# One fused kernel of attention and two expert layers: 16-bit rows between the layers, and the last unit's slots filled

## The chip, the cores and the metric

The kernel is one program on one core of a Trainium2 chip. It is written in a language in which a scheduler places semaphores and buffers; where the code asks for it, the order of an engine's instructions is the written order, otherwise a planner chooses it. The metric is device microseconds of one execution, median of several. PE is TensorE, DVE VectorE, ACT ScalarE, POOL GpSimd, SP SyncE, which issues most transfers.

## What is computed

A gated linear attention runs over 4 x 8 heads, 768 steps, head size 48. Its rows (3072 tokens, 384 wide) go through a dense two-layer network, and its output through one of eight experts per token:

```python
def _moe_ref(x, w_in, w_out):
    h = x @ w_in                      # 3072 x 384 @ 384 x 2048
    g = np.maximum(0.01 * h, h)
    return (g @ w_out)

def _moe2_ref(x, w_gate, w1, w2):     # 8 experts, 384 -> 1024 -> 384
    logits = x @ w_gate
    expert_idx = np.argmax(logits, axis=1)
    ...                               # probs: softmax of the logits
    gate_w = probs[np.arange(N), expert_idx]
    for e in range(E):
        mask = expert_idx == e
        out[mask] = gate_w[mask, None] * (np.maximum(x[mask] @ w1[e], 0) @ w2[e])
```

## The kernel before

Products are made in 16-bit parts: an operand is split into a high and a low float16, and a product is three matmuls (high-high, high-low, low-high).

**Units.** The 3072 tokens are eight units of 384 (`NU`, `UT`), numbered 0 to 7. A unit's attention is cut into `front` (decays, a scan of six levels in place in the one buffer `Ft`, logarithm and exponent, a Newton step, scaled k and q) and `back` (states, scores, outputs, the turned rows `xT`). The dense network of a unit is `moe1`: 16 slots of `products` and `leaky` (first half), then 18 slots of `stage2` (three groups of 128 rows, six slots each). `run_slots` runs the generators of other work one step a slot beside it: a step that yields n waits n slots. Units 0 and 1 start in another way: unit 0's dense layer and unit 1's attention are woven in `first`, where the planner chooses the order. From unit 1's dense layer on, PE, DVE, ACT and POOL keep the written order; SP doesn't.

**state["at"]** tells how far the dense layer is: u in its first half, u + 0.5 in its second. `fronts` lets the attention front of unit u begin when it has reached u - 1.5; `backs` follow. `first_weights` begins once the last unit's attention is done, in the second half of unit 6.

**Rows between the layers.** `finish_out` scales a group's output from PSUM (`po`) into `xg`, and `route` finds expert and place for each token, writes the rows to `x2_rows` in DRAM and scatters token numbers into `tok_list`. `tile_table` makes 28 tiles of 128 tokens (`NM`), the first 14 (`NA`) from units 0 to 6 alone. For tile j, `token_list` reads its list (SP), `gather` its rows (an indirect transfer from POOL) and `turn` transposes them into `XT` (PE, ACT, DVE).

**Experts.** `experts` goes through the 28 tiles four times (`NPH`), with a quarter of the hidden width each time: `stage` copies an expert's first weights to a fixed place (DVE), `hidden`, `relu_hi`, `relu_lo`, `combine`, `accumulate`. The weights of pass p + 1 come during pass p (`load_phase`, 32 slices of 128 x 384, 192 KB each, in a ring of `wr` buffers) and are split in two parts; those of pass 0 come with `first_weights`. Where `on_dve` says so, the low part is made by DVE, else GpSimd scales the slice and subtracts. Lists and tables of the last unit (`last_tiles`) run beside the first pass.

## Time and profile before

| | us |
|---|---|
| median of three runs | 910.66 (906.37 to 915.27) |
| the profiled execution | 912.01 |
| its span, first to last instruction | 910.3 |
| unit 1's dense layer, 163.5 to 245.9 | 82.4 |
| unit 2's, 245.9 to 309.4 | 63.5 |
| last unit's, and up to the first expert product, 559.1 to 641.7 | 82.6 |
| first pass through the experts, 641.7 to 728.9 | 87.2 |
| second pass, 728.9 to 785.5 | 56.6 |

How to read it: TensorE is busy 90% of the span (816.9 us), VectorE 72%, ScalarE 57%, GpSimd 55%. A busy table has a row for a stretch: its ends and length, then the busy us of PE, PEld (weight loads), DVE, ACT and POOL with the number of instructions, the granted clock of TensorE (1 is full), the share of the DMA engines and GB/s. A group row has line, engine, operation, written<-read names, shape and count, then busy us and mean ns of one, then the idle time of that engine just before and what ended it. A timeline row has start and length in us, engine, line, operation, names, count, and in brackets the idle time before and what ended it. "<-issue" is a wait that the trace puts down to no other engine; SPq is SyncE issuing a transfer.

### The profile page before, as it was taken

Reading aid. Unit: us, or ns where it says so; the run is one execution under the profiler, and the core shown is the slowest. Engines: PE = TensorE matmul, PEld = TensorE weight load, DVE = VectorE, ACT = ScalarE, POOL = GpSimd, SP = SyncE. Lnnn points to the kernel's source line nnn. Section 1 sums busy time; section 2 is a strip of 40 time slices with the busy share of each in tenths; the row PEclk is TensorE's granted clock in tenths of the full one; section 3 lists DMA queues with packets and bytes.
Section 4 is the critical chain, followed back from the end, with each engine's and each line's share of the span. In section 5 each row is a group of like instructions: output and inputs, shape, how many; then the busy total and the mean of one; then the engine's idle time right before and its main releaser. Section 6 shows DMA issues by size and latency. Waiting matters only on the chain.

```text
span 910.3 us, 20348 instructions
## 1 busy us (share of the span) xinstructions
PE 816.9 (90%) x7015; PEld 583.1 (64%) x7015; DVE 654.8 (72%) x1594; ACT 520.4 (57%) x1425; POOL 497.4 (55%) x575
## 2 busy tenths in 40 slices
PE   5978899959999999999999997992488899999995
PEld 3654588637677676676776664551466677777884
DVE  8899964667856766657559665655766998887774
ACT  4656755555667565575574663523346767677342
POOL 6366852254273463472552650652239879899453
PEclk8879799979999999999999999997789999999998
DMA  9573261123211212212100016225326434343121
GB/s 246 134 180 79 75 168 45 28 52 80 54 27 46 60 27 54 53 28 53 27 1 28 1 35 119 56 70 166 89 53 167 141 97 123 106 123 106 63 91 63
DMA packets 150748, 73.16 MB, mean 80 GB/s; under 512 B 108651, under 2 KB 144563, under 8 KB 150640
## 3 DMA queue, kind: packets, MB, share of 16 engines
q1 hardware_dynamic: 146176, 61.40, 26.7%
q0 software_dynamic: 4464, 10.38, 3.9%
q8 instruction: 60, 0.98, 0.5%
q14 instruction: 48, 0.39, 0.2%
HBM read 62.18 MB, written 10.36 MB: 80 GB/s over the span
## 4 chain that ended last, share of the span: by engine, by line
PE 65%; DVE 17%; issue 7%; ACT 4%; DMA 3%; POOL 2%; SPq 2%; DVEq 0%; POOLq 0%; ACTq 0%
PE m L825 15%; PE m L848 15%; PE a L1325 10%; PE m L1351 10%; PE a L319 3%; DMA wr<-in_moe_w 2%; PE a L676 2%; PE m L308 2%; DVE gf L835 2%; DVE Ft L543 1%; DVE W L1049 1%; PE a L704 1%; DVE Ft L347 1%; PE a L655 1%; PE a L468 1%
## 5 line engine op out<-in xcount | busy, mean ns | idle before, releaser
L825 PE MATMUL m<-xT,wih 128*128 128x384 f16 x1152 | 207.6, 336 | 8.2 <-DVE gf L835 7.6
L848 PE MATMUL m<-woh,gh 128*128 128x392 f16 x1152 | 205.0, 329 | 4.9 <-issue 2.1
L841 POOL TENSOR_TENSOR gh<-gf,gh 128x384 f16<-128x384 f32 x128 | 122.4, 963 | 127.4 <-ACT gh L840 127.2
L825 PEld LDWEIGHTS <-wih 128*128 128x128 f16 x1152 | 114.4, 101 | 83.7 <-issue 18.5
L1325 PE MATMUL a<-XT,st 128*128 128x128 f16 x2016 | 133.9, 222 | 34.7 <-DVE st L1296 32.8
L848 PEld LDWEIGHTS <-gh 128*128 128x128 f16 x1152 | 112.0, 99 | 76.6 <-issue 6.0
L1325 PEld LDWEIGHTS <-st 128*128 128x128 f16 x2016 | 122.0, 99 | 52.2 <-DVE st L1296 40.8
L835 DVE SCALAR_TENSOR_TENSOR gf<-m,gf 128x384 f32<-128x384 f32 x128 | 70.9, 554 | 89.7 <-ACT gf L834 85.4
L1351 PE MATMUL m<-W,hs 128*128 x672 | 128.2, 328 | 0.0
L840 ACT CAST gh<-gf 128x384 f16<-128x384 f32 x128 | 65.4, 511 | 64.5 <-DVE gf L835 62.1
L1095 POOL TENSOR_TENSOR W<-wr,W 128x384 f16<-128x384 f32 x88 | 84.5, 960 | 29.3 <-ACT W L192 21.6
L834 ACT ACTIVATE gf<-m 128x384 f32<-128x384 f32 x128 | 62.4, 487 | 50.5 <-PE m L825 41.8
L192 ACT ACTIVATE W<-wr 128x384 bf16<-128x384 f32 x128 | 66.4, 519 | 38.5 <-DMA wr<-in_moe_w 38.3
L1296 DVE COPY st<-W 128x1536 f16 x112 | 81.1, 724 | 2.7 <-issue 1.2
L1351 PEld LDWEIGHTS <-hs 128*128 128x128 f16 x672 | 61.5, 98 | 29.7 <-issue 0.7
L1076 POOL TENSOR_SCALAR wr<-wr 128x384 f32<-128x384 f32 x88 | 59.9, 682 | 27.3 <-DMA wr<-in_moe_w 26.4
L1337 DVE SCALAR_TENSOR_TENSOR hs<-a,hs 128x256 f16<-128x256 f32 x112 | 47.1, 421 | 27.7 <-ACT hs L1333 18.1
L1333 ACT ACTIVATE hs<-a 128x256 f16<-128x256 f32 x112 | 41.9, 374 | 38.3 <-PE a L1325 37.3
L319 PE MATMUL a<-ident,nat 128*128 128x128 f32 x288 | 44.8, 292 | 20.1 <-issue 9.9
L1093 ACT CAST W<-wr 128x384 f16<-128x384 f32 x88 | 44.9, 510 | 30.7 <-POOL wr L1076 29.6
L979 POOL DMA_INDIRECT tok_list<-con,pi x24 | 25.7, 1071 | 59.2 <-DVE xg L974 53.6
L1364 DVE SCALAR_TENSOR_TENSOR acc<-m,acc 128x384 f32<-128x384 f32 x84 | 51.7, 615 | 4.5 <-PE m L1351 0.7
(253 smaller groups left out, 1407.1 us busy)
## 6 DMA issues: line engine op xcount, KB each, us to landing
wr<-in_moe_w SPq DMA_DIRECT2D x128, 192.0 KB
raw_in<-in_moe_w_in SPq DMA_DIRECT2D x12, 512.0 KB
raw<-in_moe_w_out SPq DMA_DIRECT2D x16, 384.0 KB
x_rows<-xg SPq DMA_DIRECT2D x24, 193.0 KB
nat<-in_alpha SPq DMA_DIRECT2D x24, 192.0 KB
nat<-in_k SPq DMA_DIRECT2D x24, 192.0 KB
nat<-in_q SPq DMA_DIRECT2D x24, 192.0 KB
vt<-in_v SPq DMA_DIRECT2D x24, 192.0 KB
```

The lines of the kernel that those rows point to most:

```text
L192: A.activation(scrap, src, AF.Square, scale=scale, accum_out=g_sq[:, i : i + 1])
L319: T.transpose(pt[:, c * P : (c + 1) * P], nt[:, c, pr].rearrange("p z d -> p (z d)"), ident)
L825: T.matmul(ph[:, 0:UT], wih[:, a, kk, f * P : (f + 1) * P], xT[:, b, kk, :], start=(n == 0), stop=(n == 8),)
L834: A.activation(gf, ph[:, 0:UT], AF.Copy, scale=0.01 * CG)
L835: V.scalar_tensor_tensor(gf, ph[:, 0:UT], CG, gf, ALU.mult, ALU.max)
L840: A.copy(g[f][:, 0], gf)
L841: G.tensor_tensor(out=g[f][:, 1], in0=gf, in1=g[f][:, 0], op=ALU.subtract)
L848: T.matmul(po[:, 0:ROW], g[f][:, a, c * P : (c + 1) * P], woh[:, b, f, :], start=(n == 0), stop=(n == 3 * NF - 1),)
L1095: G.tensor_tensor(out=lo, in0=raw, in1=hi, op=ALU.subtract)
L1296: V.tensor_copy(out=sth[i % 2].rearrange("p a k f -> p a (k f)"), in_=Wp[ph][0][:, :, ds(reg(V, j), 1), :, :].rearrange("p a e k f -> p a ...
L1325: T.matmul(hp[:, f * P : (f + 1) * P], st[:, a, kk, f * P : (f + 1) * P], XT[j][:, b, kk, :], start=(n == 0), stop=(n == 8),)
L1351: T.matmul(yp[:, 0:DM], hs[:, a, i, :], W2[:, b, ds(rp, 1), i, :].rearrange("p e f -> p (e f)"), start=(n == 0), stop=(n == 5),)
```

## The change

Rows are stored in two float16 parts in the same bytes (`x16`): the copy out of PSUM writes the high part (`upper`), and a VectorE instruction one slot later the low part (`lower`). `turn` transposes six 16-bit blocks and copies them once. The first 15 steps of unit 2's front are taken ahead of the written order, right behind `first`; the Newton steps stand one step earlier. Fronts begin at u - 1.6, and `state["at"]` goes to u + 0.4 after 12 slots. Lists, gathers and turns of the first 14 tiles go one a slot in the last unit, three slots apart; `other_turns` is gone. The ring of weight buffers has nine in place of four; in unit 6 every fourth slice is followed by the next without a slot between, and in the last unit the slices pause until its second half. In pass 0 all 32 slices of pass 1 are split on VectorE and ScalarE, none on GpSimd; 8 were before.

```diff
--- before.py
+++ after.py
@@ -48,8 +48,7 @@
 C1 = 1.0 / (2.0 * SA * SB * CG)
 C2 = C1 / (2.0 * SW * SW)
 EXPM = 0x7F800000
-T0 = 3
-DV = 4, 1
+RING = 9
 AHEAD = (0, 0, 0)
 WARM = (45,2,2,6,4)
 LV, Y1 = 2, 9.0
@@ -579,12 +578,13 @@
             for m, sl in ((ml, slice(0, 64)), (mr, slice(64, 128))):
                 V.scalar_tensor_tensor(D5[:, pr, :, sl], pt[:, :, sl], by, m[:, pr, :, sl], ALU.mult, ALU.mult)
 
+        newton(0)
+        yield 1
+        newton(1)
+        yield 1
         vs = lp[0].tile([P, 2, 3, DM], F16, tag="vs", name="vs", bufs=1)
         r["vs"] = vs
-        newton(0)
         k0 = [tp(nk, 0), tp(nk, 1)]
-        yield 1
-        newton(1)
         G.tensor_scalar(vt, vt, YV, 1.0, ALU.mult, ALU.mult)
         yield 1
         for pr in range(2):
@@ -875,6 +875,8 @@
         g = {}
         state["at"] = u
         for f in range(NF):
+            if f == 12:
+                state["at"] = u + 0.4
             ph = products(f, xT)
             next_slot()
             gf = leaky(ph)
@@ -905,6 +907,7 @@
         e1 = res["e1"]
         xg = rt.tile([P, XR], F32, tag="xg", name="xg", bufs=4)
         rows.append(xg)
+        x16 = xg[:, 0:DM].bitcast(F16)
 
         def scale():
             mx = pm.tile([P, 1], F32, tag="mx", name="mx", bufs=2)
@@ -912,7 +915,14 @@
             s2, e2 = pow2(mx, K2, 1, "n2")
             V.tensor_scalar(L[:, c, :], po[:, DM:ROW], e1[c], C1 / res["ys"], ALU.mult, ALU.mult)
             V.scalar_tensor_tensor(gsc[:, c : c + 1], e1[c], C2 / res["ys"], e2, ALU.mult, ALU.mult)
-            when(1, lambda: A.activation(xg[:, 0:DM], po[:, 0:DM], AF.Copy, scale=s2))
+            when(1, partial(upper, s2))
+
+        def upper(s2):
+            A.activation(x16[:, 0:DM], po[:, 0:DM], AF.Copy, scale=s2)
+            when(1, partial(lower, s2))
+
+        def lower(s2):
+            V.scalar_tensor_tensor(x16[:, DM : 2 * DM], po[:, 0:DM], s2, x16[:, 0:DM], ALU.mult, ALU.subtract)
 
         when(2, scale)
 
@@ -1069,7 +1079,7 @@
                 raws.append((raw, *(W2[:, a, e, i, :] for a in range(2))))
 
         def on_dve(n):
-            return ph == 0 or (ph == 1 and n % DV[0] < DV[1])
+            return ph < 2
 
         def scaled(n):
             if n < NW and not on_dve(n):
@@ -1157,6 +1167,11 @@
         yield t
 
     weave(first(), [wo_steps, then(pause(AT0), attn(1, ld[1], res[1]))], 1.5)
+
+    ld[2] = attn_load(2)
+    first_front = front(2, False)
+    for _ in range(15):
+        next(first_front)
     everything = {getattr(mybir.EngineType, e) for e in ("PE", "Activation", "DVE", "Pool")}
     pe_order.enter_context(tc.manual_schedule(engines=everything))
     tm_ctx.close()
@@ -1187,9 +1202,9 @@
 
     def fronts():
         for u in range(2, NU):
-            while state["at"] < u - 1.5:
+            while state["at"] < u - 1.6:
                 yield 1
-            yield from front(u, u == 2)
+            yield from first_front if u == 2 else front(u, False)
             state["front"] = u
             yield 1
 
@@ -1223,12 +1238,17 @@
         acc.extend(pw.tile([P, XR], F32, name=f"acc{j}") for j in range(NA))
         sth.append(pw.tile([P, 2, 3, FQ], F16, name="st0"))
         n = 0
-        for _ in load_phase(0, pw, pw, 4):
+        for _ in load_phase(0, pw, pw, RING):
             n += 1
             if n % 2 == 0:
-                yield 1 if state["at"] % 1 else 4
-
-    ld[2] = attn_load(2)
+                if state["at"] < NU - 1:
+                    if n % 8:
+                        yield 1
+                else:
+                    yield 1
+                    while state["at"] < NU - 0.5:
+                        yield 1
+
     halves = fronts(), backs()
     sides = [[0, g] for g in (*halves, first_weights())]
 
@@ -1257,32 +1277,26 @@
         )
 
     def turn(j):
-        px = pst("a")
-        for kk in range(3):
-            T.transpose(px[:, kk * P : (kk + 1) * P], acc[j][:, kk * P : (kk + 1) * P], ident)
-        pxv = px[:, 0:DM].rearrange("p (k t) -> p k t", k=3)
-        A.copy(XT[j][:, 0], pxv)
-        after(lambda: V.tensor_tensor(out=XT[j][:, 1], in0=pxv, in1=XT[j][:, 0], op=ALU.subtract))
+        px = pst("a").bitcast(F16)
+        x16 = acc[j][:, 0:DM].bitcast(F16)
+        for kk in range(6):
+            T.transpose(px[:, kk * P : (kk + 1) * P], x16[:, kk * P : (kk + 1) * P], ident16)
+        A.copy(XT[j].rearrange("p a k t -> p (a k t)"), px[:, 0 : 2 * DM])
 
     def full_tiles():
         yield 3
         yield from route(NU - 2, res[NU - 2])
         yield 1
         yield from tile_table(0, NA)
-        for j in range(NA):
-            token_list(j)
-        yield 3
-        for j in range(NA):
-            gather(j)
-            if 8 <= j < 8 + T0:
-                turn(j - 8)
+        for j in range(NA + 6):
+            if j < NA:
+                token_list(j)
+            if 3 <= j < NA + 3:
+                gather(j - 3)
+            if j >= 6:
+                turn(j - 6)
+                state["turned"] = j - 6
             yield 1
-
-    def other_turns():
-        for j in range(T0, NA):
-            turn(j)
-            state["turned"] = j
-            yield 2.0
 
     regs = {}
 
@@ -1363,7 +1377,7 @@
         else:
             V.scalar_tensor_tensor(ac, yp[:, 0:DM], gt, ac, ALU.mult, ALU.add)
         if ph == NPH - 1:
-            junk = pw.tile([P, DM], F32, tag="wr", name="junk", bufs=4)
+            junk = pw.tile([P, DM], F32, tag="wr", name="junk", bufs=RING)
             A.activation(junk, ac, AF.Copy, scale=0.0, accum_out=g_out[:, j : j + 1])
             if j == 0:
                 G.drain()
@@ -1399,7 +1413,7 @@
 
     def weights(ph):
 
-        it = load_phase(ph + 1, pw if ph % 2 else m2, pw, 4) if ph + 1 < NPH else iter(())
+        it = load_phase(ph + 1, pw if ph % 2 else m2, pw, RING) if ph + 1 < NPH else iter(())
         for j in range(NM):
             if j:
                 next(it, None)
@@ -1417,7 +1431,7 @@
         n = NPH * NM
         for i in range(n + 3):
             while i < NM and state["turned"] < i:
-                next(turns if i < NA else lists, None)
+                next(lists, None)
                 while late:
                     late.pop(0)()
             if i < n:
@@ -1440,8 +1454,7 @@
             yield
 
     lists = last_tiles()
-    turns = other_turns()
-    weave(experts(), [turns, lists], 2.0)
+    weave(experts(), [lists], 2.0)
     pe_order.close()
 
 
```

## Rows read from the trace of the kernel before

**Rows 1.** Busy table by stretch: us (count) per engine, clock, DMA share, GB/s.
```profile
100.00:163.50 63.50, 61.93 (x462) 48.15 (x463) 39.63 (x91) 36.96 (x109) 32.91 (x49) 0.95 0.35 93
...
163.50:245.90 82.40, 70.32 (x548) 49.12 (x547) 60.62 (x168) 48.48 (x127) 34.94 (x33) 0.94 0.25 51
...
245.90:309.40 63.50, 63.50 (x507) 43.95 (x507) 43.52 (x125) 38.86 (x99) 31.16 (x32) 1.00 0.22 46
...
559.10:641.70 82.60, 53.02 (x305) 29.90 (x302) 51.73 (x145) 32.29 (x93) 32.01 (x34) 0.89 0.39 108
...
641.70:728.90 87.20, 68.88 (x731) 54.54 (x732) 68.71 (x165) 50.70 (x150) 54.18 (x65) 0.93 0.42 111
...
728.90:785.50 56.60, 56.60 (x682) 44.25 (x680) 47.88 (x86) 41.17 (x124) 51.31 (x64) 1.00 0.39 112
```
**Rows 2.** Timeline around unit 1's attention; columns as told above.
```profile
118.34 0.35 DVE L371 SCALAR_TENSOR_TENSOR qt<-a,Ft 128x192 f32<-128x192 f32 x1
...
193.33 1.51 PE L319 MATMUL a<-ident,nat 128*128 128x128 f32 x6 [9.89 <-issue]
```
**Rows 3.** Groups of 163.5 to 245.9 (unit 1); columns as told above.
```profile
L543 DVE TENSOR_TENSOR Ft<-Ft 128x384 f32<-128x384 f32 x24 | 16.1, 720 | 0.0
...
L319 PE MATMUL a<-ident,nat 128*128 128x128 f32 x72 | 10.8, 285 | 9.9 <-issue 9.9
...
L575 DVE SCALAR_TENSOR_TENSOR R<-ln,R 128x768 f32<-128x768 f32 x4 | 5.0, 1249 | 0.1
```
**Rows 4.** Timeline of the last unit and the hand-over, all engines.
```profile
557.56 0.52 ACT L192 ACTIVATE W<-wr 128x384 bf16<-128x384 f32 x1 [9.04 <-DMA wr<-in_moe_w]
...
568.80 7.69 PE L825 MATMUL m<-xT,wih 128*128 128x384 f16 x36 [5.13 <-DVE gf L835]
...
601.30 18.98 SPq L1249 DMA_DIRECT2D tok<-tok_list  x14
...
623.44 0.52 ACT L192 ACTIVATE W<-wr 128x384 bf16<-128x384 f32 x1 [20.36 <-DMA wr<-in_moe_w]
...
641.14 0.56 DVE L1296 COPY st<-W 128x1536 f16 x1 [0.54 <-DVE W L1049]
...
641.75 2.10 PE L1325 MATMUL a<-XT,st 128*128 128x128 f16 x18 [18.96 <-DVE st L1296]
```
**Rows 5.** Groups of 641.7 to 728.9, the first pass through the experts.
```profile
L1325 PE MATMUL a<-XT,st 128*128 128x128 f16 x500 | 35.4, 229 | 34.6 <-DVE st L1296 32.8 <-DVE acc L1362 0.8 <-ACT XT L1264 0.8
...
L1095 POOL TENSOR_TENSOR W<-wr,W 128x384 f16<-128x384 f32 x24 | 22.6, 943 | 19.8 <-ACT W L192 19.7
...
L1296 DVE COPY st<-W 128x1536 f16 x28 | 21.6, 772 | 1.6 <-issue 1.2 <-DVE acc L1362 0.3
...
L1265 DVE TENSOR_TENSOR XT<-a,XT 128x384 f16<-128x384 f32 x25 | 13.7, 549 | 12.2 <-ACT XT L1264 10.4 <-ACT W L192 1.8
...
L1262 PE MATMUL a<-ident,acc 128*128 128x128 f32 x75 | 13.4, 289 | 2.6 <-DVE XT L1265 2.3 <-issue 0.2
...
L1430 DVE SCALAR_TENSOR_TENSOR W<-wr,W 128x384 f16<-128x384 f32 x8 | 5.7, 710 | 0.6 <-ACT W L1088 0.6
```
**Rows 6.** Timeline of the first pass through the experts.
```profile
648.54 1.18 PE L1325 MATMUL a<-XT,st 128*128 128x128 f16 x18 [1.49 <-DVE st L1296]
...
660.62 2.10 PE L1325 MATMUL a<-XT,st 128*128 128x128 f16 x18 [6.60 <-DVE st L1296]
...
662.92 8.45 SPq L1249 DMA_DIRECT2D tok<-tok_list  x6
...
674.08 0.52 POOL L1076 TENSOR_SCALAR wr<-wr 128x384 f32<-128x384 f32 x1 [5.69 <-DMA wr<-in_moe_w]
```
**Rows 7.** Groups of the whole span: a ScalarE instruction 768 wide.
```profile
L556 ACT ACTIVATE ln<-Ft 128x768 f32<-128x768 f32 x12 | 10.0, 834 | 20.0 <-DVE Ft L543 20.0
```
**Rows 8.** Timeline of the last unit: a gather on GpSimd, a turn on TensorE.
```profile
605.71 0.98 POOL L1252 DMA_INDIRECT acc<-x_rows,tok  x1 [0.30 <-issue]
...
610.07 0.49 PE L1262 MATMUL a<-ident,acc 128*128 128x128 f32 x3
```

More of the change, by code (lines that the diff above doesn't have):

```diff
@@ L273, in tile_kernel @@
     lp = [pm]
-    state = {"S": None, "SU": None, "e": None, "nat": 0, "sm": 0, "wo": 0, "turned": T0 - 1, "at": 0, "attn": 1, "front": 1}
+    state = {"S": None, "SU": None, "e": None, "nat": 0, "sm": 0, "wo": 0, "turned": -1, "at": 0, "attn": 1, "front": 1}
     qeng = [nc.sync, nc.scalar]
@@ L1519, in last_experts @@
             G.indirect_dma_start(out=x, out_offset=None, in_=x2d, in_offset=rows)
+            x16 = x[:, 0:DM].bitcast(F16)
+            xs = le.tile([P, DM], F32, name="l_xs")
+            V.tensor_tensor(out=xs, in0=x16[:, 0:DM], in1=x16[:, DM : 2 * DM], op=ALU.add)
             px = pst("a")
             for kk in range(3):
-                T.transpose(px[:, kk * P : (kk + 1) * P], x[:, kk * P : (kk + 1) * P], ident)
+                T.transpose(px[:, kk * P : (kk + 1) * P], xs[:, kk * P : (kk + 1) * P], ident)
             xT = le.tile([P, 3, P], F32, name="l_xT")
```

## The prediction

> **What bounds the kernel now.** I read the busy table by stage first [rows 1]. In units 2 to 5 (one shown, 245.9 to 309.4) TensorE is busy all of the time at the full granted clock, with VectorE at 43.5 of 63.5 us: nothing taken from another engine is worth anything there. The second pass through the experts (728.9 to 785.5, 28 tiles in 56.6 us, 2.02 us each) is bound by TensorE in the same way. TensorE loses time in three places. Unit 1 takes 82.4 us with 70.3 busy, 12.1 idle. The last unit with the hand-over to the experts takes 82.6 with 53.0 busy, 29.6 idle. The first pass through the experts takes 87.2 with 68.9 busy, 18.3 idle. These 60 us are what the change can take from; the rest is start and tail.
>
> Next the timeline of each hole, to see which wait ends last. Unit 1: VectorE runs the scan of unit 2, six levels of two multiplications at 0.72 us, then the Newton steps [rows 3]; the products with k come after them in its queue, and TensorE's transposes for q need the PSUM buffers that these set free: idle 9.9 us until 193.3 [rows 2]. Last unit: SyncE issues 14 token lists in one go, 18.98 us from 601.3 [rows 4]. The expert weights stand behind them in its queue, so ScalarE sits 20.36 us, and the first stage copy, emitted behind every weight slice, comes at 641.1 after a TensorE wait of 18.96 us. TensorE also lost 5.13 us at 568.8 to a `gf` that stood on VectorE behind weight work. First pass: TensorE waits 34.6 us ahead of its weight-and-token product, 32.8 of it for the stage copy [rows 5], so what ends last is VectorE's queue: 68.7 us busy, and 12.2 idle ahead of the subtraction of `turn`, which waits for a ScalarE that stood behind GpSimd's scaling, which stood behind a weight transfer (5.69 us at 674.1), issued behind six token lists (8.45 us from 662.9) [rows 6].
>
> **The change, part by part.** *Unit 2's scan, traced in unit 0's stage.* It takes out of unit 1's queues 12 transposes on TensorE (12 x 0.15, 1.8 us), eight copies on ScalarE, half of the 24 level instructions on VectorE (12 x 0.72, 8.6 us) and half of the Newton steps (four at 1.25, 5 us) [rows 3]. VectorE in unit 1 goes from 60.6 to about 47, TensorE needs 70.3 - 1.8 = 68.5, so TensorE should be the bound as in unit 2. Of the 12.1 us idle I keep 3. Where it goes: the scan's buffer `Ft` is free once unit 1's q is scaled, at 118.7 [rows 2], and over 100 to 163.5 VectorE has 23.9 us free, most of it after that [rows 1]: 13.6 fit. TensorE there is full (61.9 of 63.5), so the transposes cost their 1.8 us again, and I take 1 more for attention steps of unit 1 delayed on VectorE. Gain 9.1 + 1.8, cost 2.8, -8; the clock (granted 0.94 in unit 1, 1.00 in unit 2) gives an estimated 2 back: **-10**. Bounds: no idle left and all hidden, -14; the scan put at the end of unit 0 and half exposed, -4.
>
> *Two 16-bit parts.* `lower` is new, 24 times on VectorE. No row shows it; the subtraction in `turn` has the same operand kinds and takes 0.55 us (13.7 us for 25 [rows 5]); bounds 0 and the 0.71 of a `lo`. It holds the PSUM buffer `po` a slot longer and stands ahead of the next `gf`. In the units TensorE is the cover, with 20 us of VectorE free: 0. With that cover gone it costs 24 x 0.55 = 13 us. The three at the hand-over may cost 0.5.
>
> *Turns.* Three 32-bit transposes, a copy and a subtraction become six 16-bit transposes and one copy of 768. A turn costs TensorE 0.54 now (13.4 us for 25 [rows 5]). Six 16-bit ones are not shown: below, 18 products of the same width take 1.18 us [rows 6], so 0.39; above, six at the 32-bit price, 1.07. I take 0.45, near the row of the same type and width. The copy I take at the 0.83 of a 768 wide one [rows 7], bounds half and all of it. VectorE loses the 25 subtractions and their waits.
>
> *Lists, gathers, turns and weights in the last unit's slots.* The first weights start three slots earlier in unit 6 (a slot is 63.5/34 = 1.87 us) and go four slices to three slots; by my count of the yields 18 of 32 are done when the last unit begins, one more in its first slot, and none until its second half. So in slots 15 to 34 SyncE has the lists almost to itself, and with nine buffers the transfers of later slices are issued ahead of the lists. Of the 29.6 us idle I expect 1.5 in place of the 18.96, 3 of the 5.13 and its like, and 1 of the rest. TensorE's own work is 53.0 plus 14 turns less the three there now (14 x 0.45 - 3 x 0.54 = 4.7). Sum 53.0 + 4.7 + 5.5 = 63.2, less 1.2 for the clock (granted 0.89): 62 against 82.6, **-20.6**. Bounds: 57.7 with no idle at all (-25); 72, if half of the idle stays (-10). VectorE pays two instructions of up to 0.71 us a slice and ScalarE a square and 0.83 a turn, against slots of 1.87: covered.
>
> *First pass without GpSimd.* GpSimd loses 22.6 us of subtractions and its scalings; 24 more slices put a `lo` of 0.71 us on VectorE [rows 5]: +17.0. VectorE: 68.7 - 13.7 + 17.0 = 72.0 busy; of 18.5 idle the 12.2 ahead of the turn's subtraction go, 6.3 stay: 78. The stage copy has a mean of 0.77 here against 0.56 for one at 641.1 [rows 4]; GpSimd, with which it was drawn out, falls from 54.2 us to under 32: 28 copies at 0.1 less, 75. TensorE: 68.9 - 25 x 0.54 + 14 x 0.45 = 61.7, plus 12 for the waits on the last rows' routing and tables, which stay (6.60 us at 660.6 [rows 6] is the largest): 74. Both say 74.5 against 87.2: **-12.7**. Bounds: 64 and 90.
>
> The Trainium skill (SBUF — State Buffer, "Who interferes with whom") has GpSimd and VectorE's copies lock each other out of shared ports for a whole instruction; by that rule all that a stage copy has over 0.56 us would go, some 3 us more than I count. The same page (its "DVE blocks DMA" trap) speaks against gathers beside VectorE's copies, since GpSimd writes their descriptors. Gathers beside such copies in the last unit follow each other at 0.30 us [rows 8]; the trace does not bear the trap out here, and I charge nothing.
>
> Sum: -10 - 20.6 - 12.7 + 0.5 = -42.8. The profiled execution has 912.0 us (span 910.3 and 1.7 around it), the median of the runs is 910.66: **869**.
>
> **The rivals.**
> *Weights still late (881).* The four slices in flight at 548 took until 557.6, with ScalarE 9.04 us idle [rows 4]: 2.3 us a slice. At that rate 18 slices take 41 us, and their slots in unit 6 last 24; the queues of ScalarE and VectorE carry the delay into the last unit's `gf`, and some 12 of the 20.6 us stay lost. Against it: four buffers allowed no more in flight, and nine do.
> *VectorE keeps the first pass (885).* If its idle time stays beside the added work, 72.0 + 18.5 = 90: the 12.7 us are not gained and 3 are lost.
> *The scan is not hidden (878).* The order in unit 0's stage is left to the planner, which may place the scan behind unit 0's last work; then unit 1's first `gf` stand behind it and 9 of the 10 us go.
> *Everything opens (854).* No idle left in unit 1 and the hand-over (4 + 4.4), the stage copy at its best and the tables overlapped (7).
> *The first three together (906):* 869 + 12 + 16 + 9, within 1% of now.
> *Slower (925).* Turns now stand in TensorE's own order in the last unit, each behind its list, its gather and two landings. If a gather's data comes later than the three slots given to it, each of 14 turns stops the matmuls: above (42.8 + 9.1)/14 = 3.7 us a turn the change is slower by over 1%, and at 4.0 it is 925. Against it: a gather issued until 606.7 is turned at 610.1 without a wait [rows 8], 3.4 us, and three slots are 4.5 to 6.
>
> **How the numbers follow.** Forecast 0.55; weights late 0.15; VectorE 0.10; everything opens 0.07; scan not hidden 0.06; the three together 0.04; slower 0.03. A measurement of this kernel can tell about 1% from no change, 901.6 to 919.8 here: faster 0.93, same 0.04, slower 0.03. The likeliest case's own range is 855 to 881. The range 846 to 893 takes in the bounds of the hand-over and of the first pass and all cases but the last two.
>
> **What would show it.** Right: no long gap of TensorE in unit 1, and unit 1 near 70 us; scan instructions before 163; the first expert product within 3 us of the last unit's end; lists on SyncE one by one; ScalarE never 5 us on a weight slice in the last unit; GpSimd with gathers and scatters alone in the first pass, and 28 tiles there in about 75 us. Wrong: scan levels after 165, `gf` waits over 5 us at the last unit's start, turns with a wait on a gather, or VectorE over 95% busy in the first pass. What would overthrow the forecast is a new wait of over 20 us on TensorE in the last unit.

## The result and the profile after

The changed kernel takes 899.58 us (median), the kernel before 910.66 beside it: a ratio of 0.989, interval 0.986 to 0.993. The forecast was 869, with 846 to 893. The direction was right; of the 42 us of gain forecast against that median, 11 came.

The busy table by stretch, of the kernel after: us, busy time and count of TensorE, its weight loads, VectorE, ScalarE and GpSimd, granted clock, DMA share, GB/s. The stretches are the end of unit 0, unit 1, unit 2, the last unit with the hand-over, and the first and second pass through the experts.

```profile
100.00:160.80 60.80, 59.66 (x465) 47.09 (x463) 38.63 (x94) 34.90 (x104) 29.32 (x46) 0.99 0.36 95
160.80:246.00 85.20, 70.40 (x540) 48.67 (x538) 60.16 (x170) 47.68 (x125) 34.65 (x35) 0.94 0.25 49
246.00:309.20 63.20, 63.20 (x507) 43.84 (x505) 42.10 (x126) 38.61 (x99) 30.40 (x31) 1.00 0.24 45
559.10:633.10 74.00, 60.03 (x380) 35.77 (x379) 43.51 (x123) 35.70 (x87) 31.64 (x33) 0.88 0.39 110
633.10:713.60 80.50, 66.12 (x744) 52.64 (x742) 62.59 (x164) 50.74 (x141) 18.45 (x19) 0.89 0.41 117
713.60:770.00 56.40, 56.40 (x679) 44.11 (x677) 50.20 (x87) 41.16 (x124) 49.43 (x61) 1.00 0.39 114
```

Against [rows 1]: unit 1 is 2.8 us longer, not 10 shorter. The hand-over fell from 82.6 to 74.0 (forecast 62), the first pass from 87.2 to 80.5 (forecast 74.5). The second pass has not moved. In unit 1 VectorE is as busy as before and TensorE has the same two losses, 14.8 us of idle (12.1 before) and a clock of 0.94. The profiled execution took 895.93 us, 3.7 less than the median. The timeline of unit 1 after (start, us, engine, line, operation, out<-in, count, idle before and its releaser) says why.

```profile
164.31 5.23 DVE L542 TENSOR_TENSOR Ft<-Ft 128x384 f32<-128x384 f32 x11
...
169.54 0.55 DVE L835 SCALAR_TENSOR_TENSOR gf<-m,gf 128x384 f32<-128x384 f32 x1
...
173.84 2.52 DVE L574 SCALAR_TENSOR_TENSOR R<-ln,R 128x768 f32<-128x768 f32 x2
...
176.29 0.54 DVE L835 SCALAR_TENSOR_TENSOR gf<-m,gf 128x384 f32<-128x384 f32 x1
...
177.46 1.51 PE L318 MATMUL a<-ident,nat 128*128 128x128 f32 x6 [10.44 <-issue]
```

Unit 2's scan, which was to run in unit 0's stage, runs with its Newton steps from 163.2 to 176.3, in unit 1. It stands behind unit 0's last work, as the code emits it; unit 1's `gf` stand behind it in VectorE's order, and TensorE's gap is the old one (9.9 us in [rows 2]) 16 us earlier. The last unit and the first pass, on the same timeline:

```profile
566.50 3.69 PE L825 MATMUL m<-xT,wih 128*128 128x384 f16 x13 [2.88 <-DVE gf L835]
...
599.45 1.16 POOL L1272 DMA_INDIRECT acc<-x_rows,tok  x1 [2.20 <-DMA tok<-tok_list]
...
603.16 0.80 PE L1283 MATMUL a<-ident,acc 128*128 128x128 f16 x6 [6.68 <-DMA acc<-x_rows,tok]
...
615.09 0.33 PE L848 MATMUL m<-woh,gh 128*128 128x392 f16 x1 [0.91 <-issue]
...
616.51 0.33 PE L848 MATMUL m<-woh,gh 128*128 128x392 f16 x1 [1.10 <-issue]
...
617.24 0.49 PE L848 MATMUL m<-woh,gh 128*128 128x392 f16 x1 [0.40 <-issue]
617.94 0.50 PE L848 MATMUL m<-woh,gh 128*128 128x392 f16 x1 [0.22 <-issue]
...
619.45 0.80 ACT L1284 COPY XT<-a 128x768 f16<-128x768 f16 x1 [5.87 <-remote]
...
652.19 2.10 PE L1339 MATMUL a<-XT,st 128*128 128x128 f16 x18 [5.21 <-DVE st L1310]
...
678.98 0.22 PE L1283 MATMUL a<-ident,acc 128*128 128x128 f16 x1 [0.52 <-issue]
...
679.71 0.27 PE L1283 MATMUL a<-ident,acc 128*128 128x128 f16 x2 [0.51 <-issue]
```

Three things are to be seen. The 18.96 us wait for the stage copy [rows 4] is gone, and ScalarE's 20 us on a weight slice with it. In their place TensorE waits 6.7 us at the first turn for its gather. And from 613.8 to 619.3, and again at 671 and from 678 to 682, TensorE starts an instruction only every 0.7 us or slower: matmuls that wait for nothing stand alone, 0.7 to 1.4 us apart, and ScalarE starts nothing for 5.9 us ("<-remote" is a release that the trace places on no engine). I call this slow issue. The busy table of the stretch, with one before and one behind it:

```profile
605.00:613.40 8.40, 8.40 (x64) 5.48 (x63) 4.08 (x12) 4.53 (x12) 5.13 (x6) 0.88 0.67 173
613.40:620.00 6.60, 3.08 (x15) 1.06 (x13) 1.35 (x3) 0.73 (x3) 3.65 (x5) 0.79 0.69 193
620.00:628.00 8.00, 8.00 (x54) 5.16 (x53) 5.82 (x16) 6.95 (x17) 0.76 (x1) 0.75 0.64 188
```

Last, groups of the first pass after (busy us, mean ns | idle before, releasers):

```profile
L1339 PE MATMUL a<-XT,st 128*128 128x128 f16 x501 | 36.3, 231 | 13.0 <-DVE st L1310 10.0 <-PE a L1283 1.9 <-issue 0.9
...
L1310 DVE COPY st<-W 128x1536 f16 x28 | 16.1, 575 | 3.1 <-DVE acc L1376 1.8 <-issue 1.1
...
L1284 ACT COPY XT<-a 128x768 f16<-128x768 f16 x16 | 12.7, 794 | 4.3 <-PE a L1283 4.2
```

The DMA engines are no busier in the slow stretch (0.69) than before (0.67) and behind it (0.64), so their load alone does not mark it. The wait ahead of the expert product fell from 34.6 to 13.0 us [rows 5]; the stage copy fell from a mean of 772 to 575 ns; the turn's copy is 794 ns, 830 forecast.

### The profile page after: what moved, and what is told of

Same layout as the page of the kernel before. It is cut to its first block, busy times and chain, and to the rows that moved or that the text cites. A ratio compares the mean times of both kernels' runs of the same rounds, so it can differ in the third digit from the quotient of the medians.

```text
span 893.8 us, 20449 instructions
## 1 busy us (share of the span) xinstructions
PE 817.0 (91%) x7099; PEld 584.7 (65%) x7099; DVE 653.3 (73%) x1614; ACT 527.2 (59%) x1425; POOL 458.6 (51%) x527
## 4 chain that ended last, share of the span: by engine, by line
PE 74%; DVE 12%; issue 4%; ACT 4%; DMA 3%; POOL 3%; DVEq 0%; SPq 0%; POOLq 0%; ACTq 0%
PE m L848 16%; PE m L825 16%; PE a L1339 13%; PE m L1365 12%; PE a L318 3%; PE a L676 2%; PE a L655 1%; PE a L1283 1%; DMA wr<-in_moe_w 1%; DVE gf L835 1%; PE a L704 1%; DVE Ft L346 1%; PE a L712 1%; PE a L467 1%; DVE w L1513 1%
## 5 line engine op out<-in xcount | busy, mean ns | idle before, releaser
L848 PE MATMUL m<-woh,gh 128*128 128x392 f16 x1152 | 207.1, 332 | 3.5 <-issue 3.5
L1365 PE MATMUL m<-W,hs 128*128 x672 | 130.3, 332 | 0.0
L1105 POOL TENSOR_TENSOR W<-wr,W 128x384 f16<-128x384 f32 x64 | 61.6, 963 | 20.3 <-ACT W L191 16.3
L1086 POOL TENSOR_SCALAR wr<-wr 128x384 f32<-128x384 f32 x64 | 44.7, 700 | 22.8 <-DMA wr<-in_moe_w 22.7
L318 PEld LDWEIGHTS a<-ident,nat 128*128 128x128 f32 x288 | 36.6, 148 | 23.3 <-issue 12.9
```

The lines of the kernel that those rows point to most:

```text
L318: T.transpose(pt[:, c * P : (c + 1) * P], nt[:, c, pr].rearrange("p z d -> p (z d)"), ident)
L848: T.matmul(po[:, 0:ROW], g[f][:, a, c * P : (c + 1) * P], woh[:, b, f, :], start=(n == 0), stop=(n == 3 * NF - 1),)
L1105: G.tensor_tensor(out=lo, in0=raw, in1=hi, op=ALU.subtract)
L1365: T.matmul(yp[:, 0:DM], hs[:, a, i, :], W2[:, b, ds(rp, 1), i, :].rearrange("p e f -> p (e f)"), start=(n == 0), stop=(n == 5),)
```

## Experiments

Kernels timed side by side on one chip, with the kernel before among them, form a set. All ratios are to the kernel before in the same set. "First pass" runs from the first expert product to the second pass's first stage copy, "hand-over" from the last unit's first product to the first expert product. In the cuts of code, `...` marks what is left out, and words behind # are added here.

### The scan

**scan_mid.** The scan's steps are emitted in between those of unit 1's attention.

```diff
...
-    weave(first(), [wo_steps, then(pause(AT0), attn(1, ld[1], res[1]))], 1.5)
...
-    ld[2] = attn_load(2)
     first_front = front(2, False)
-    for _ in range(15):
-        next(first_front)
...
+    def lead():
+        while state["q"] < 1:        # set in attn() behind scaled(nq, qt, R5, F5)
+            yield 0.5
+        ld[2] = attn_load(2)
+        for _ in range(15):
+            next(first_front)
+            yield 2.0
...
+    weave(first(), [wo_steps, then(pause(AT0), attn(1, ld[1], res[1])), lead()], 1.5)
```

> The changed kernel with the first steps of unit 2's scan emitted between the steps of unit 1's attention, from the moment that attention has scaled q, and no longer behind it. Theory (the move was worth nothing only because the planner put the scan behind unit 0's last work): scan levels before 150, unit 1 from 85 to 70 to 74 us, TensorE's 10.4 us gap there gone, whole time 8 to 11 us under the changed kernel's 899.6, near 890 and 0.978 of before. Rival (unit 0's stage is full, what is put there comes out behind it): unit 0's stage grows by 8 to 13 us, whole time within 3 us of 899.6.

874.37 us, 0.961 (0.958 to 0.964). Unit 0 and unit 1 of it, and the first of its scan levels:

```profile
66.60:166.20 99.60, 88.83 (x629) 63.94 (x627) 85.65 (x179) 65.97 (x197) 57.66 (x72) 0.96 0.36 90
166.20:239.10 72.90, 68.69 (x539) 48.06 (x538) 50.95 (x154) 43.13 (x105) 34.24 (x35) 1.00 0.25 46
...
142.13 0.55 DVE L543 TENSOR_TENSOR Ft<-Ft 128x384 f32<-128x384 f32 x1
```

The theory holds in what the trace shows: a scan level at 142.1, unit 1 at 72.9 us with 4.2 idle and the clock at 1.00; unit 0's 99.6 lie among the 98.3 to 101.6 that executions with the scan behind it take. The whole time was expected near 890 and is 25 us under the 899.58 of the first measurement; more than half of that has another cause, since this set has no slow issue (after_third, below). What the scan's place is worth shows within the set: scan_back, with the scan in unit 1, takes 886.12, turn_late, with the scan behind unit 0, 885.09; so 11 to 12 us. The idea of the change was worth its 10 us; the place at which the scan is emitted lost them.

**scan_back.** The scan back in unit 1.

```diff
-    first_front = front(2, False)
-    for _ in range(15):
-        next(first_front)
...
-            yield from first_front if u == 2 else front(u, False)
+            yield from front(u, u == 2)
```

> The changed kernel with unit 2's scan back in unit 1, as before the change; all else as changed. Theory (the move of the scan gained nothing): whole time within 3 us of the changed kernel's 899.6, unit 0 and unit 1 together 179 to 182 us against 186 after and 179 before from the first product of unit 0. Rival (the move did gain in unit 0 or later and the loss came from another part): 6 to 10 us over 899.6.

886.12 us, 0.977 (0.973 to 0.981). That looks like a gain of 13 us over 899.58. The trace contradicts it: scan_back shows no slow issue, and the changed kernel itself came to 886.9 in a set without it (after_third, below). Against that, and against 885.09 for turn_late in the same set, the move was worth nothing, as expected. Units 0 to 2 together take 248.0 us here, 247.7 in after_third, 242.4 before: so the change costs some 5 us there with the scan in either place. I moved nothing else of that part, so the cause (fronts that begin at the 13th product, the Newton steps spread over more slots) stays open.

```profile
60.00:156.60 96.60, 87.85 (x616) 63.55 (x615) 74.25 (x155) 60.93 (x175) 54.22 (x71) 0.95 0.34 87
156.60:240.10 83.50, 70.54 (x540) 48.80 (x539) 63.41 (x167) 47.03 (x125) 34.52 (x32) 0.96 0.25 46
240.10:308.00 67.90, 65.55 (x515) 45.28 (x515) 46.65 (x136) 39.84 (x101) 34.68 (x35) 1.00 0.24 45
```

### Slow issue

**after_again, after_third.** The changed kernel unedited, in two other sets.

> The changed kernel as it is, a second time. Theory (the stretches at 614 to 620 and 671 to 682, in which all engines issue one instruction in 0.7 us, belong to the chip or the execution and not to the kernel, since four near relatives show none): none of them, hand-over near 70 and first pass near 73 us against 74.0 and 80.5, whole time 886 to 891. Rival (they belong to this kernel's own times of gathers): the stretches again, whole time 897 to 902.

902.02 us, 0.992 (0.989 to 0.995), slow issue again, hand-over 74.4 and first pass 80.0: the rival's numbers. Its reason, that the stretches belong to this kernel, does not stand up to the next run.

> The changed kernel as it is, as a measure for the others of this set. With the stretches of slow issue: 897 to 903, hand-over 74, first pass 80. Without: 885 to 891, hand-over 70, first pass 73.

886.9 us, 0.975 (0.969 to 0.981), on the same chip as after_again, and no slow issue anywhere. Its last unit and first pass:

```profile
560.10:627.70 67.60, 57.56 (x383) 35.17 (x381) 42.91 (x122) 36.27 (x87) 32.33 (x33) 0.92 0.43 123
627.70:699.60 71.90, 63.55 (x744) 51.95 (x742) 61.56 (x164) 50.21 (x141) 18.42 (x19) 0.91 0.46 131
...
604.06 0.80 PE L1283 MATMUL a<-ident,acc 128*128 128x128 f16 x6 [6.70 <-DMA acc<-x_rows,tok]
```

So one kernel on one chip has two times 15 us apart (13 against the first measurement), alike within a set. Three sets had slow issue (the first measurement, that of after_again, that of ring4), three had not (one of these, that of lists_static_2, without the unedited kernel in it). The kernel before has little of it (some 2 us at 614 to 619 in its profile, where TensorE's weight loads come 0.7 us apart): 910.6 to 911.0 in the sets with, 908.3, 908.6 and 910.9 in those without. Two of its rows:

```profile
616.56 0.10 PEld L848 LDWEIGHTS <-gh 128*128 128x128 f16 x1 [0.61 <-issue]
...
617.28 0.26 PEld L848 LDWEIGHTS <-gh 128*128 128x128 f16 x2 [0.62 <-issue]
```

**spread.** Gathers drawn apart, in a set whose near kernels (pace_back, x16_back) show slow issue; the unedited kernel was not in that set. In the first pass the second edit draws lists and turns apart too.

```diff
     def gather(j):
+        for _ in range(3):
+            G.tensor_scalar(fill, fill, 1.0, 1.0, ALU.mult, ALU.mult)
         G.indirect_dma_start(
...
-            yield 1.0        # in last_tiles()
+            yield 2.0
```

> The changed kernel with gathers drawn apart: three small operations of GpSimd, 0.2 us or so each, ahead of every gather, and the last rows' lists, gathers and turns at half the pace in the first pass. Theory A (gathers one behind the other hold up the issue on all engines): on a chip where such stretches appear in the changed kernel, at most 2 us of them are left, whole time 5 to 9 us under the changed kernel's 900 to 902 there; where they do not appear, within 3 us. Rival B (lists, or the amount of transfers): the stretches stay, whole time within 3 us.

899.1 us, 0.987 (0.981 to 0.994). No slow issue; gathers are 2.5 to 3.1 us apart, against 1.2 to 1.6 for three to eight in a row ahead of every such stretch in the others.

```profile
565.70:645.60 79.90, 58.90 (x381) 34.44 (x379) 46.17 (x130) 36.72 (x89) 47.96 (x75) 0.91 0.37 103
645.60:718.00 72.40, 64.13 (x744) 52.37 (x743) 61.83 (x158) 50.16 (x140) 37.60 (x61) 0.88 0.47 130
...
633.16 0.51 PE L1288 MATMUL a<-ident,acc 128*128 128x128 f16 x6 [1.87 <-DMA acc<-x_rows,tok]
```

The first pass falls to 72.4 us, as theory A wants. The hand-over grows to 79.9: at that distance the gathers fall behind the turns, and behind the first, which waits 7.0 us, nine more wait 0.4 to 1.9 us each. So the whole time stays, where theory A expected 5 to 9 us less, by another mechanism than either theory named.

**lists_static, gather_plain.** List addresses as constants; plain transfers of 128 rows in order in place of gathers, so that the experts get other rows than theirs.

```diff
-        ro = nc.sync.value_load(off[0:1, j : j + 1], min_val=0, max_val=E * CAP)
-        nc.sync.dma_start(out=tok[:, j : j + 1], in_=lst[ds(ro, P), :])
+        e, t = LISTS[j]
+        nc.sync.dma_start(out=tok[:, j : j + 1], in_=lst[e * CAP + t * P : e * CAP + t * P + P, :])
```

```diff
-        G.indirect_dma_start(out=acc[j], ...)
+        t0 = j * P if j < NA else NTOK - (NM - j) * P
+        G.dma_start(out=acc[j], in_=x2d[t0 : t0 + P, :])
```

> The changed kernel with each gather by a list replaced by a plain transfer of 128 rows in order, of the same size and from the same queue; the token lists are still loaded but the experts work on the wrong rows. Theory A (gathers by a list, one behind the other, hold up the issue of instructions on all engines at once, some 5.5 us at 614 to 620 and some 5.7 at 671 to 682): no stretch in which TensorE issues one instruction in 0.7 us, the first pass from 80.5 to 75 us, the hand-over 5 us shorter. Rival B (the list loads with an address from a register do it, or so many transfers of any kind at once): such stretches stay, with 4 us or more in all.

> The changed kernel with plain transfers of 128 rows in place of the gathers, a second time, beside the changed kernel on the same chip; the experts work on the wrong rows. Theory A (gathers by a list): no stretch of slow issue, first pass 72 to 73 us, whole time 8 to 13 us under the changed kernel of the set where that has the stretches. Rival C (the amount of transfers of any kind): stretches of 4 us or more stay.

> The changed kernel with plain transfers in place of gathers, a third time, beside the one with fixed list addresses; the experts work on the wrong rows. Theory A: no stretch of slow issue, first pass 72 to 75 us, 884 to 889, also where its neighbour shows them. Rival C (close transfers of any kind): stretches as in its neighbour, 894 or more.

> The changed kernel with the 28 token lists loaded from addresses written into the program (those that the tables give for this data) and not from registers; so a list no longer waits for the table. Theory A (gathers by a list make the slow issue): stretches of 0.7 us a step stay, 4 us or more in all, where the changed kernel of the same set has them. Rival B (the register loads, with SyncE's address work, make it): none left. In both the first turn's wait of 6.6 us shrinks below 3, since its list comes earlier.

> The changed kernel with the token lists loaded from addresses written into the program, a second time, in a new set. Theory A (close gathers by a list make the slow issue, in some sets): if the set has it, stretches of 4 us or more and 894 to 900 us. Rival B (the register loads make it): none, 883 to 887. If the kernel beside it and this one both show none, nothing follows.

gather_plain 884.44, 888.41 and 885.88 us, lists_static 885.15 and 887.37, none with slow issue, but no neighbour in their sets had it either. So they don't tell A from B or C. They show one thing: the hand-over is 66.4 to 68.0 us in these runs, whether a list waits for its table or not, and whether a transfer waits for a list or not. With plain transfers, mostly 0.53 us apart, the first turn still waits 3.7 to 3.8 us and no later one waits, but the wait for a `gf` at the unit's start is 4.8 to 5.0 us where it was 2.7. That the first turn's wait would fall below 3 us with early lists was wrong (4.6).

### Which part brought the gain

Each part of the change was taken back alone, in sets with slow issue. The changed kernel stands at 0.989 and 0.992 in such sets; it was timed beside pool_back and slots_back, but not in the set of ring4, pace_back and x16_back.

```diff
-        return ph < 2                     # pool_back
+        return ph == 0 or (ph == 1 and n % 4 < 1)
-RING = 9                                  # ring4
+RING = 4
-                if state["at"] < NU - 1:  # pace_back, with the loop under it
+                yield 1 if state["at"] % 1 else 4
```

slots_back puts `full_tiles` and `other_turns` back as they were, x16_back puts `finish_out` and `turn` back.

> The changed kernel with GpSimd scaling and subtracting three of four weight slices in the first pass, as before the change. Theory (taking GpSimd off is what brought the first pass from 87 to 73 us, since VectorE's queue ended last there): first pass 80 to 87 us, whole time 7 to 14 us over the changed kernel of the same set. Rival (the turns and lists taken out of the first pass brought it, and GpSimd's work was hidden): first pass under 76, whole time within 2 us.

899.57 us, 0.989 (0.983 to 0.994): 2.5 us under the changed kernel of the set, near what the rival has, but not for its reason. The first pass is 79.2 us against 80.0 in the same set, without slow issue in it, though the hand-over of the same execution has it (615 to 620): GpSimd's scalings and subtractions hold the first pass's gathers 1.9 to 4.2 us apart.

```profile
632.20:711.40 79.20, 62.70 (x743) 49.69 (x741) 57.77 (x140) 50.51 (x141) 53.53 (x62) 0.94 0.45 117
...
L1310 DVE COPY st<-W 128x1536 f16 x27 | 18.7, 694 | 2.0 <-DVE acc L1376 0.8 <-issue 0.8
```

Against 71.7 to 73.3 us for the pass where gathers stand close and no slow issue comes, taking GpSimd off is worth 6 to 7 us, and in sets with slow issue that is given back: the gathers then close up, and slow issue comes. The stage copy has a mean of 694 ns with GpSimd busy and 575 without. By the Trainium skill (SBUF — State Buffer, "Who interferes with whom") copies of VectorE in a two-port mode and GpSimd's instructions lock each other out; the two means agree with that.

> The changed kernel with the lists issued in one go, the gathers behind them, three turns in the last unit and eleven in the first pass, as before the change; weights, two 16-bit parts and the rest as changed. Theory (the slots gave the hand-over its 9 to 13 us by letting weights past the lists): hand-over 78 to 83 us, first pass 76 to 80, whole time 10 to 15 us over the changed kernel of the same set. Rival (the earlier weights and the nine buffers gave it alone): hand-over under 72 us, whole time within 4 us.

898.1 us, 0.988 (0.982 to 0.995): the rival's numbers. Hand-over 69.6, first pass 82.0, both with slow issue. But ScalarE waits 8.3 us on a weight slice at 622.0 here, and TensorE 5.6 us for the first stage copy, which it does not in the changed kernel: nine buffers alone do not take all weights past the lists.

> The changed kernel with four buffers for raw weight slices in place of nine. Theory (what the hand-over gained came from weights that no longer stand behind the lists, and the nine buffers are what lets them be issued ahead): a wait of ScalarE on a weight slice of 5 us or more in the last unit, hand-over 5 to 9 us longer than with nine (74.0 and 74.4 in two executions), whole time 4 to 9 us longer. Rival (the earlier pacing of the slices gave it, four buffers would do): hand-over within 2 us, whole time within 3 us.

903.75 us, 0.995 (0.992 to 0.998): 2 to 5 us longer, at the theory's lower end. In the last unit ScalarE waits at most 1.4 us on a slice; the cost shows as TensorE's 5.0 us wait at 570.6 and in the hand-over, 72.6 without a slow step, against 67.6 in after_third.

```profile
631.50:713.70 82.20, 63.74 (x745) 50.62 (x743) 62.22 (x163) 50.62 (x141) 17.13 (x18) 0.94 0.41 114
...
L191 ACT ACTIVATE W<-wr 128x384 bf16<-128x384 f32 x32 | 16.9, 527 | 12.4 <-DMA wr<-in_moe_w 12.3
```

The first pass shows more: one slow step (678.8), and yet 82.2 us against 71.9 in after_third, with nearly the same busy times of TensorE and VectorE. ScalarE waits 12.3 us on slices there, 1.1 in after_third. So by these two profiles the nine buffers are worth some 5 us in the hand-over and 10 in the first pass where slow issue stays away; the whole time of this set hides it, since the changed kernel pays slow issue in their place.

> The changed kernel with the first pass's weights paced as before the change (none ahead of the list slots by rule, every other one in four slots of a unit's first half). Theory (the earlier weights gave the hand-over most of its 9 us): slices left behind the last unit's end, hand-over 78 us or more, whole time 4 to 9 us longer. Rival (nine buffers alone give it): hand-over within 2 us of 74, whole time within 3 us.

899.52 us, 0.988 (0.984 to 0.992): the rival; hand-over 73.6, with slow issue in it, as in the first pass (82.8).

> The changed kernel with x2 stored as one 32-bit part: turns of three 32-bit transposes, a copy and a subtraction again, and no second part computed in the units. Theory (the 16-bit turns save 14 subtractions of 0.55 us on VectorE and 0.04 to 0.1 us of TensorE a turn, both mostly beside other work): whole time 1 to 5 us longer, the first pass 2 to 4 us longer. Rival (the subtraction, behind a ScalarE copy, stops VectorE as it did before the change, 12.2 us idle): first pass 7 us or more longer.

901.68 us, 0.993 (0.990 to 0.997): not to be told from the changed kernel's 0.989 and 0.992. The first pass is 3.5 to 4 us longer than theirs, as the theory has it, with 14 subtractions back on VectorE:

```profile
636.50:720.50 84.00, 69.24 (x704) 54.62 (x705) 66.00 (x177) 45.70 (x140) 18.47 (x19) 0.86 0.39 112
```

In whole time no part undone alone costs more than 5 us, though the whole brought hand-over and first pass 15 us each (after_third). That is no measure of a part where undoing it also takes slow issue away, as pool_back (6 to 7 us in the first pass) and ring4 (5 and 10) show. Whether the other parts stand in for each other is not shown: pairs of parts, and parts in a set without slow issue, weren't tried.

### The hand-over, and all together

**turn_late.** The turns of the last unit three slots later (`range(NA + 9)`, `turn(j - 9)`).

> The changed kernel with each of the 14 turns of the last unit three slots later in TensorE's order, lists and gathers as they are. Theory (the 6.7 us that TensorE waits at the first turn for its gather are lost time of their own): that wait under 2 us, first expert product 4 to 6 us earlier after the last unit's start (74.0 us now), whole time 4 to 6 us under 899.6. Rival (weights or the slow issue of all engines end last there): the wait goes but the first expert product comes at the same time, whole time within 2 us.

885.09 us, 0.974 (0.971 to 0.977), without slow issue; so to be held against 886.9.

```profile
607.94 0.50 PE L1283 MATMUL a<-ident,acc 128*128 128x128 f16 x6 [2.51 <-DMA acc<-x_rows,tok]
...
563.00:630.80 67.80, 57.64 (x380) 34.79 (x378) 45.36 (x129) 36.56 (x89) 32.41 (x33) 0.94 0.42 123
```

The first turn's wait fell from 6.7 to 2.5 us and the hand-over stayed at 67.8: my theory falls. The rival has the time right, but neither weights nor slow issue end last: the last three turns now wait 1.1, 0.8 and 1.0 us for their gathers, which they don't in after_third, and the `gf` at the unit's start 3.7 in place of 2.7.

**mid_and_late** is scan_mid with turn_late, in a set with slow issue. **best1** is scan_mid with turns four slots later and the last rows' lists at half the pace, in one without.

> The changed kernel with both: unit 2's scan emitted between the steps of unit 1's attention, and the last unit's turns three slots later. Theory (separate losses, they add): 3 to 5 us under the first of the two alone (874.4), 868 to 872. Rival (the later turns gained nothing of their own): 873 to 876.

883.78 us, 0.973 (0.966 to 0.980). The expectation, made from 874.4 in a set without slow issue, can't be held against a set with it (first pass 81.0). Against the changed kernel of its own set it is 18 us less, more than the scan's 11 to 12: the hand-over is 69.7 here and 74.4 there, both with slow issue, so later turns may gain up to 5 us in such a set. That rests on one profile each.

> The changed kernel with unit 2's scan emitted between the steps of unit 1's attention, the last unit's turns four slots later, and the last rows' lists, gathers and turns at half the pace in the first pass. Theory (three separate losses): on a chip with slow issue 875 to 880 (883.8 with the first two alone on such a chip, less the 5 us of slow issue in the first pass), on one without 866 to 872. Rival (half the pace makes tiles wait for their turns, or the slow issue goes with the number of gathers and not with their distance): 882 to 888 on a chip with slow issue.

874.15 us, 0.960 (0.954 to 0.966): the same as scan_mid alone, and 2 us above the 866 to 872 that the theory of separate losses gave for such a set. mid_and_late and best1 are faster than the kernel before and the changed one. The last turns of best1 wait instead of its first:

```profile
599.14 0.49 PE L1289 MATMUL a<-ident,acc 128*128 128x128 f16 x6 [1.05 <-DMA acc<-x_rows,tok]
...
617.53 0.53 PE L1289 MATMUL a<-ident,acc 128*128 128x128 f16 x6 [1.41 <-DMA acc<-x_rows,tok]
619.58 1.58 PE L1289 MATMUL a<-ident,acc 128*128 128x128 f16 x12 [1.52 <-DMA acc<-x_rows,tok]
...
553.30:621.00 67.70, 57.05 (x380) 34.36 (x379) 45.54 (x129) 36.32 (x89) 32.25 (x33) 0.93 0.44 123
```

Where turns stand later, the row of 14 gathers behind the tables ends last: the last turns wait for the last gathers.

## Why the prediction was wrong, step by step

| stretch, us | before | forecast | after | after_third | scan_mid |
|---|---|---|---|---|---|
| up to unit 0's first product | 66.8 | as before | 60.0 | 62.6 | 66.6 |
| units 0 and 1 | 179.1 | 169.1 | 186.0 | 184.5 | 172.5 |
| units 2 to 6 | 313.2 | as before | 313.1 | 313.1 | 313.1 |
| last unit and hand-over | 82.6 | 62 | 74.0 | 67.6 | 70.0 |
| first pass | 87.2 | 74.5 | 80.5 | 71.9 | 73.0 |
| from there on | 181.4 | as before | 180.2 | 180.3 | 180.3 |

**The scan: the failed step.** I charged *the scan is not hidden* 9 us and gave it 0.06; it came true in full. The argument counted VectorE's free time behind 118.7 and took for granted that the planner would use it. It had no row on the planner's order, and the emission, which the diff does show, stands behind all of unit 1's attention. The size was right: where the scan is hidden (scan_mid), unit 1 is 72.9 us against some 70 forecast, with the 68.7 of TensorE's work (68.5) and the clock at 1.00, and the whole is 11 to 12 us under its neighbours in the set; unit 0 pays 3.0 us for it (99.6 against 96.6 in scan_back), forecast at 2.8. On top the change costs some 5 us in units 0 to 2 that I had not seen, so that units 0 and 1 of scan_mid gain 6.6 us on the kernel before and not 10.

**The hand-over: the term was mis-sized.** TensorE's own work was forecast at 57.7 and is 57.6 (after_third). Idle was put at 5.5 and is 10: 2.7 at a `gf`, for which 3 was put down, and 6.7 at the first turn, which was put at nothing. I had weighed only gather to turn, 3.4 us against three slots. The first list waits for the table as well: list at 596.5, gather at 599.5, data at 603.1. Nor is that wait to be had back by itself, since turns set later gained nothing without slow issue: then the last gathers end last. *Weights still late* did not come: in the changed kernel ScalarE waits at most 1.9 us on a slice from 545 to the first expert product (20.4 before), though by 559.1 it had begun 13 slices and not the 18 that I counted (6 before). With the lists in one go (slots_back) it still waits 8.3 us.

**The first pass: right where no slow issue disturbs it.** 71.7 to 73.3 us against 74.5. Of the two paths that gave the forecast, TensorE's is borne out: 63.6 busy and 8.4 waiting (after_third), for 61.7 and 12. VectorE's came near the same number by luck: its busy time was put at 69 and is 61.6, since a `lo` takes 0.55 us without GpSimd (L1444, put at 0.71) and the stage copy 0.58 (put at 0.67). *VectorE keeps the first pass* did not come. `lower` took 0.62 us and cost nothing in units 2 to 6, as said; a turn takes TensorE 0.50 (0.45).

**What no step held: slow issue.** In the profile of the result the hand-over is 6.4 us longer than in after_third (74.0 against 67.6) and the first pass 8.6 (80.5 against 71.9). The slow stretches themselves last 5.5 us and some 5; the rest, in the first pass with TensorE busy 2.6 us longer at a clock of 0.89 against 0.91, is not told apart. The kernel before shows it too, at 614 to 619, as weight loads 0.7 us apart with nothing to wait for; I read over it. I costed the gathers' descriptors at nothing on the strength of 0.30 us between gathers [rows 8], and looked at GpSimd alone.

**Sum.** From 42.8 us forecast: 17 missing in units 0 and 1, 12 in the hand-over, 6 in the first pass, 1 gained behind, and 7 gained ahead of unit 0's first product, which no edit touches and which differs from 59.3 to 67.6 among all kernels here. That leaves 16 of 43, as the spans say (910.3 to 893.8); the medians lie 11 apart. Without slow issue the change is worth 2.5%, and 886.9 lies within the range. Of the rivals *the first three together* (906) comes nearest in number, by luck: of its three only the scan came true.

## What to carry to other kernels

Work that is moved into a stretch ordered by a planner is moved only if it is emitted there: look for it in the new order before its gain is counted. When one transfer's wait is taken away from a chain of list, gather and turn, ask when the last of the row lands, since that is what stayed here. A part that is taken back in a disturbed set is judged by its own stretch of the trace, not by the whole time alone. And a kernel's time can differ by more than the change between two sets on one chip, so a variant is held against the kernel it came from in the same set, and its trace is searched for stretches in which several engines slow at once.

## What the runs showed of the hardware

Slow issue was not expected: for 1 to 6 us at a time TensorE, SyncE and the others start an instruction only every 0.7 us (or 1.4), waits or not, while GpSimd's gathers go on; it begins after three to eight gathers at 1.2 to 1.6 us distance, in some sets and not in others. It was absent wherever gathers stood 1.9 us or more apart (the first pass of pool_back, whose last unit has it, and all of spread). That close gathers are a condition is supported by this; that they are the cause, and what makes one set differ from the next on the same chip, stays open, and so does whether register loads or plain transfers have a part. Between 613.4 and 620 the trace of the changed kernel lists no transfer of instructions, so a late one does not explain that stretch.

Beside GpSimd's scaling and subtracting, VectorE's instructions on weights take longer: the stage copy 694 ns and `lo` 826 in the first pass of pool_back, 575 and 552 in that of the changed kernel.
